# RWKV-6 attention and a squared-ReLU MLP in one kernel: source parity as row half of the score tiles, state in compact 64x64 tiles

## Chip, cores and metric

One core of one Trainium2 chip runs the whole kernel in one launch. The metric is the device time of an execution in microseconds (us), compared by medians of runs. Besides these times there is one profiled execution, from which the profile and the trace come.

## What is computed

For each batch and head a recurrence with a decay per token and channel, then an MLP over all tokens:

```python
B, H, S, D = 4, 8, 768, 48          # r, k, v, w: (B, H, S, D); u: (H, D)
for t in range(S):
    cur = einsum('bhd,bhe->bhde', u * k_t, v_t)
    y_t = einsum('bhd,bhde->bhe', r_t, state + cur)
    state = w_t[..., None] * state + einsum('bhd,bhe->bhde', k_t, v_t)
x = y.transpose(0, 2, 1, 3).reshape(3072, 384)
out = relu(x @ w_in) ** 2 @ w_out   # w_in: 384 x 2048, w_out: 2048 x 384, float32 in and out
```

## The kernel before

**Tiling.** Work goes in 12 steps `s` of 256 tokens: four batches of three steps each, so steps 0, 3, 6 and 9 begin with an empty state. A partition holds a pair of neighbouring tokens, with parity `j`, so a step is 128 pairs; they make two chunks `c` of 64 pairs (`Q`). Heads go in four pairs `p` of two heads `e`, each padded from 48 to 64 channels, so that a head pair fills 128 rows. A step's parts are loaded by `ld.s.x` (x is w, r, k or v, 384 KB each, four buffers for each part); `ld.g.i` and `ld.g.o` load the blocks of the two MLP weights, which `cast` turns to bf16.

**The operations of a step**, by their names in the program:
- `ww_`, `lw_`, `cum_`, `exp_`, `ac_`: the pair's decay, its logarithm (ScalarE), sums along the chunk by triangular matmuls on TensorE, exponentials, and each chunk's total decay. `rw_`, `kw_` multiply r and k by one token's decay; `rd_` multiplies r (i = 0) and k (i = 1) by the decays.
- `tr_` with `rkt_` (steps 0 to 3) or `dtr_` (steps 4 to 11) transpose them: by TensorE and a copy, or by a transposing DMA of SBUF. `rkT` holds both.
- `p_`: the scores, pairs of k against pairs of r, in 64x64 tiles of the array; `pm_` masks them on VectorE. Rows of a score tile are the 64 source pairs of chunk 0 and below them of chunk 1; the source parity `js` is a place in the free dimension.
- `su_` (k times v), `ts_` (adds the old state), `sn_` (multiplies by the decay): the state after each chunk. It is kept for a head pair as 128 rows by 96 columns, of which only the two diagonal blocks are wanted: zeros in `ac_buf` clear the others.
- `y_` (scores times v, in array tiles of 64 rows by 128 columns), `yc_` (r times the state, 128 by 64): the output in PSUM.
- `ku_`, `qp_`, `q_`, `vq_`: the term with u, a number q per token and head that multiplies v. It enters y through `yq_` (a matmul with `spread`) or, in steps 4 and 7 to 11, through `dvq`: four DMAs bring it to the output's layout, and `ysb_` adds it.
- `ysb_`, then `yt_` with `xt_` or the transposing DMA `dyt_`: the MLP's input `xT`.
- `m1_` (first layer, six matmuls of 256 columns, two PSUM banks in turn), `rl_` (ReLU), `sq_` (square), `m2_` (second layer, four of 384 columns), `os_` and `store`.

**Order.** All of it is written out in one string, `ORDER`; each engine carries out its own operations in the order in which they stand there. A word names the operation, the step, the PSUM banks after a colon, and after `=` the engine (A ScalarE, V VectorE, G GpSimd), where there is a choice. SyncE's queue (SP) issues all DMAs, loads, shuffles, transposes and stores, in that order too; an issue whose buffer or data isn't ready holds up those behind it. `warm_` words are matmuls of zeros for the time in which TensorE has nothing to do.

Of the kernel before, what the change touches and what calls it, by code (L numbers as in the profile page):

```python
# [29 lines left out]
rl_.0.5=A cast.o.1=V m2_.0.1.0:0 sq_.0.1=A cast.o.2=G cum_.3:1 q_.2 ld.3.v m1_.1.3:1 sq_.0.2=A pm_.2.0  # L30
m2_.0.0.0:1 vq_.2 sq_.1.3=A m2_.0.1.1 rl_.1.3=V m2_.0.1.2 ld.4.w v_.2=A sq_.1.1=V m1_.1.1:1 cast.o.3=A
m2_.0.0.1 rl_.1.5=V ld.4.r rl_.1.1=V m2_.0.0.2 ac_.3 m2_.0.0.3 rw_.3=V exp_.3 ld.4.k su_.2:0 sq_.1.0=A
os_.0.0=V m2_.0.1.3 ts_.2.0=V kw_.3=G rd_.3.0 m1_.1.4:0 os_.0.1=A ld.4.v m2_.1.0.0:1 sn_.2.0 rd_.3.1
m2_.1.0.1 v_.3=A ku_.3 tr_.3.0:0 ld.5.r rl_.1.4=A yy_.2:01 rkt_.3.0=V sq_.1.2=A ww_.4=V qp_.3 ld.5.k
tr_.3.1:0 ts_.3.0=V ysb_.2=A m2_.1.0.2 rkt_.3.1=V lw_.4 ld.5.w m2_.1.0.3 sn_.3.0 yt_.2:0 os_.1.0=A cum_.4:1
xt_.2=V rw_.4=G m2_.1.1.0:1 ac_.4 q_.3 exp_.4 m1_.2.2:1 kw_.4=G m1_.2.0:0 rd_.4.0 rl_.2.2=A m2_.1.1.1 ku_.4
rl_.2.0=A rd_.4.1 m1_.2.1:1 ts_.3.1=V m1_.2.3:0 dtr_.4.1 rl_.2.1=A v_.4=V vq_.3 pp_.3:10 rl_.2.3=A m2_.1.1.2
sq_.2.0=A ld.6.k pm_.3.0 m1_.2.5:1 ld.5.v sn_.3.1 pm_.3.1 ld.6.w m1_.2.4:0 rl_.2.5=A dtr_.4.0 m2_.1.1.3
sq_.2.1=A ww_.5=G m1_.2.6:1 os_.1.1=V rl_.2.4=A qp_.4 kw_.5=V yy_.3:10 sq_.2.2=A ld.6.r lw_.5 m2_.2.1.0:0
ysb_.3=A store.0.1 ts_.4.0=V m1_.2.7:0 q_.4 sn_.4.0 cum_.5:0 rl_.2.7=A yt_.3:1 rw_.5=V ld.7.w rl_.2.6=A  # L40
vq_.4 m2_.2.1.1 ac_.5 xt_.3=V m2_.2.1.2 exp_.5 ts_.4.1=V m1_.3.5:0 sq_.2.3=A rd_.5.0 ww_.6=G m2_.2.0.0:1
dvq.4 rl_.3.5=A rd_.5.1 m1_.3.1:1 m1_.3.0:0 rl_.3.1=V rw_.6=G pp_.4:10 rl_.3.0=A m1_.3.3:1 v_.5=A pm_.4.1
dtr_.5.0 ku_.6 m2_.2.0.1 lw_.6 rl_.3.3=A pm_.4.0 m2_.2.1.3 dtr_.5.1 m1_.3.7:0 ku_.5 m1_.3.4:1 ld.7.k
rl_.3.7=A yy_.4:01 store.0.0 rl_.3.4=A sn_.4.1 sq_.3.0=A ld.7.r m1_.3.6:0 ld.8.w qp_.5 ysb_.4=V os_.2.1=A
m1_.3.2:1 rl_.3.6=A ts_.5.0=V m2_.2.0.2 sq_.3.3=A rl_.3.2=V ld.6.v ww_.7=G yt_.4:0 q_.5 ld.8.r m2_.2.0.3
xt_.4=A kw_.6=G pp_.5:10 sq_.3.2=A m1_.4.1:0 pm_.5.1 qp_.6 store.1.0 m1_.4.3:1 rl_.4.1=A pm_.5.0 m2_.3.0.0:0
sq_.3.1=A ld.7.v cum_.6:0 kw_.7=G lw_.7 os_.2.0=V m1_.4.2:0 rl_.4.3=A rw_.7=V m2_.3.0.1 sn_.5.0 exp_.6
store.1.1 cum_.7:1 ac_.6 m2_.3.0.2 rd_.6.0 rl_.4.2=A vq_.5 m1_.4.0:1 exp_.7 rd_.6.1 m2_.3.0.3 ac_.7 v_.6=A
rd_.7.0 ku_.7 m1_.4.5:0 dtr_.6.1 rl_.4.0=A m2_.3.1.0:1 rd_.7.1 sq_.4.1=A m1_.4.4:1 dtr_.6.0 ww_.8=V qp_.7
os_.3.0=A yy_.5:01 q_.6 rl_.4.4=A ld.8.k sq_.4.0=A ld.9.w m1_.4.6:1 store.2.1 ysb_.5=V ts_.6.0=A m2_.3.1.1  # L50
sn_.6.0 ld.9.v rl_.4.5=V m2_.3.1.2 sq_.4.2=A ts_.6.1=V yt_.5:0 m1_.4.7:0 xt_.5=V sn_.6.1 lw_.8 m2_.3.1.3
rl_.4.7=V rl_.4.6=A kw_.8=G pp_.6:10 m1_.5.6:1 pm_.6.1 vq_.6 m2_.4.1.0:0 rl_.5.6=A pm_.6.0 m1_.5.4:0
os_.3.1=A ku_.8 v_.7=A store.3.1 m1_.5.0:1 rl_.5.4=V ld.8.v m2_.4.1.1 dtr_.7.0 yy_.6:01 qp_.8 ld.10.w
m1_.5.1:0 ts_.7.0=V ysb_.6=A dtr_.7.1 rw_.8=G m2_.4.0.0:1 sq_.4.3=A rl_.5.1=V m2_.4.0.1 sn_.7.0 q_.7 dyt_.6
rl_.5.0=A cum_.8:1 q_.8 m1_.5.3:0 vq_.7 exp_.8 ld.9.k m1_.5.7:1 ts_.7.1=V rl_.5.3=A ld.9.r rd_.8.0 m2_.4.0.2
ac_.8 v_.8=A m1_.5.2:0 rd_.8.1 dvq.7 rl_.5.7=A m2_.4.1.2 rl_.5.2=A m1_.5.5:1 sq_.5.1=V m2_.4.0.3 ww_.9=V
pp_.7:01 dtr_.8.0 rl_.5.5=V m1_.6.6:0 pm_.7.0 m1_.6.3:1 ku_.9 rl_.6.6=A ld.11.w m2_.4.1.3 pm_.7.1 store.3.0
rl_.6.3=A m1_.6.0:0 sq_.5.2=A dtr_.8.1 os_.4.1=V sn_.7.1 m1_.6.1:1 rl_.6.0=V sq_.5.0=A yy_.7:01 kw_.9=G
rl_.6.1=A lw_.9 rw_.9=G m1_.6.4:0 ts_.8.0=V ysb_.7=V m1_.6.5:1 qp_.9 rl_.6.4=A cum_.9:0 sq_.5.3=A rl_.6.5=V
dyt_.7 m2_.5.0.0:0 exp_.9 m1_.6.2:0 vq_.8 store.2.0 ac_.9 m2_.5.0.1 rd_.9.0 rl_.6.2=A ld.11.k m2_.5.0.2  # L60
ww_.10=G rd_.9.1 ld.10.r m2_.5.0.3 dvq.8 ww_.11=V m1_.6.7:1 os_.5.0=A sq_.6.2=V sq_.6.0=A pp_.8:10 rl_.6.7=V
m1_.7.1:0 os_.4.0=A m2_.5.1.0:0 lw_.10 rl_.7.1=V dtr_.9.0 m2_.5.1.1 q_.9 kw_.11=G m1_.7.7:1 dtr_.9.1 pm_.8.1
m1_.7.6:0 v_.9=G rl_.7.7=A m2_.6.0.0:1 lw_.11 sn_.8.0 pm_.8.0 ld.10.k rl_.7.6=A m1_.7.0:1 ld.11.r sq_.6.1=A
m1_.7.5:0 sq_.7.3=V sq_.6.3=A yy_.8:01 rl_.7.0=V rl_.7.5=V m2_.6.0.1 ysb_.8=V ts_.9.0=A m2_.5.1.2 sn_.9.0
# [26 lines left out]
def kernel(  # L91
# [13 lines left out]
    nc = tc.nc  # L105
# [475 lines left out]
```

## Time and profile before

| what | value |
|---|---|
| runs | 189.17, 192.50, 192.39 us; median 192.39 |
| profiled execution, first to last instruction (span) | 186.6 us; what lies around the span isn't in the profile: 5.8 us to the median |
| granted TensorE clock | 1.000 |
| busy: TensorE (PE), VectorE, ScalarE, GpSimd | 176.2, 133.7, 119.4, 103.7 us |
| DMA | 36.99 MB, mean 198 GB/s; 86.4% of 16 engines' span on SP's queue |
| first-layer matmuls (L478) | 576, 73.8 us busy |
| second-layer matmuls (L503) | 384, 72.1 us busy |
| score matmuls (L342) | 384 |
| output, carried and q*v matmuls (L395) | 384, 160 and 24 |
| state matmuls (L372) | 160 |
| DMA transposes `rkT<-rdec_buf` | 16, median 4.4 us from issue to landing |
| shuffles `vqs<-vq` | 24, median 3.6 us |

PE is TensorE's matmuls and PEld its weight loads, DVE is VectorE, ACT ScalarE, POOL GpSimd; L395 is line 395 of the kernel. Busy time is the union of the instructions' times; a matmul's duration has the passage through the array in it, so distances from start to start say more of what it costs. A line of the timeline or the chain merges neighbouring instructions of one kind.

### The profile page before, as it was taken

How to read it: one execution, taken by the hardware profiler on the slowest of the kernel's cores; microseconds unless marked ns; L12 is line 12 of the kernel's file. 1: busy time of each engine (PE TensorE's matmuls, PEld its weight loads, DVE VectorE, ACT ScalarE, POOL GpSimd, SP SyncE). 2: the span in 40 equal slices, each digit the busy share in tenths (PEclk: the TensorE clock that was granted, in tenths of full speed). 3: DMA queues.
4: the chain of work that ended last, by engine and by line, in shares of the span. 5: the costliest groups of instructions: out<-in, count | busy, mean ns of one | idle time of the engine just before them, and what ended most of it. 6: DMA issues, size and time to landing. Idle time of an engine off the chain costs nothing.

```text
span 186.6 us, 5415 instructions
## 1 busy us (share of the span) xinstructions
PE 176.2 (94%) x2284; PEld 125.4 (67%) x2284; DVE 133.7 (72%) x180; ACT 119.4 (64%) x193; POOL 103.7 (56%) x100
## 2 busy tenths in 40 slices
PE   7679979998999999999997999999999999999992
PEld 2245558865777778767766786777767877776661
DVE  4499927998589784889856958958996966705430
ACT  5447978988778877996747486738733073372431
POOL 7089944763999569995694595383673310000000
PEclk9999999999999999999999999999999999999999
DMA  6999999999998999999899999899497442403022
GB/s 151 269 282 354 317 213 345 364 313 259 243 239 192 167 284 174 280 286 172 236 208 184 236 216 255 142 191 254 144 130 169 100 109 63 87 0 126 0 88 85
DMA packets 80873, 36.99 MB, mean 198 GB/s; under 512 B 72529, under 2 KB 79313, under 8 KB 80849
## 3 DMA queue, kind: packets, MB, share of 16 engines
q1 hardware_dynamic: 80848, 36.64, 86.4%
q8 instruction: 18, 0.29, 0.7%
q14 instruction: 7, 0.05, 0.1%
HBM read 25.36 MB, written 4.72 MB: 161 GB/s over the span
## 4 chain that ended last, share of the span: by engine, by line
PE 68%; SPq 12%; DMA 8%; ACT 5%; DVE 2%; issue 1%; POOL 1%
PE bk L503 29%; PE m L478 27%; SPq L162 9%; PE att L395 5%; DMA w_st<-in_moe_w_out_dram 5%; DMA w_st<-in_moe_w_in_dram 4%; SPq L172 3%; PE att L342 3%; PE att L372 2%; ACT gt L487 2%; DVE q L274 1%; ACT v_bf L253 1%; ACT wo_sb L185 1%; POOL wi_sb L185 1%; SPq L190 1%
## 5 line engine op out<-in xcount | busy, mean ns | idle before, releaser
L478 PE MATMUL m<-xT,wi_sb 128*128 128x256 bf16 x576 | 73.8, 273 | 1.1 <-ACT gt L487 0.9
L503 PE MATMUL bk<-wo_sb,gt 128*128 128x384 bf16 x384 | 72.1, 326 | 0.6 <-ACT wo_sb L185 0.6
L478 PEld LDWEIGHTS <-wi_sb 128*128 128x128 bf16 x576 | 55.0, 98 | 14.0 <-issue 1.9
L487 ACT ACTIVATE gt<-m 128x512 f16<-128x512 f32 x57 | 33.5, 595 | 28.3 <-PE m L478 27.5
L503 PEld LDWEIGHTS <-gt 128*128 128x128 bf16 x384 | 36.9, 98 | 20.1 <-issue 0.8
L495 ACT ACTIVATE gt<-gt 128x1024 bf16<-128x1024 f16 x37 | 38.5, 1053 | 7.1 <-DVE gt L489 6.8
L489 DVE TENSOR_SCALAR gt<-m 128x512 f16<-128x512 f32 x39 | 26.2, 685 | 8.4 <-PE m L478 8.0
L355 DVE TENSOR_TENSOR pmT<-att,mask 128x1024 bf16<-128x1024 f32 x23 | 27.4, 1214 | 3.4 <-PE att L342 3.4
L265 POOL TENSOR_TENSOR ku<-k_raw,u_bc 128x768 f32<-128x768 f32 x12 | 22.1, 1848 | 9.7 <-DMA u_bc<-in_u_dram 5.0
L387 POOL TENSOR_TENSOR S<-t_state,ac_buf 128x384 bf16<-128x384 f32 x20 | 17.7, 886 | 9.9 <-ACT t_state L380 4.5
L270 POOL TENSOR_TENSOR ku<-ku,r_raw 128x768 f32<-128x768 f32 x12 | 22.3, 1864 | 0.5
L278 POOL TENSOR_TENSOR vq<-v_raw,q 128x768 bf16<-128x768 f32 x12 | 18.0, 1499 | 4.8 <-DVE q L274 4.8
L510 ACT ACTIVATE o_sb<-bk 128x384 f32<-128x384 f32 x15 | 7.3, 487 | 11.9 <-PE bk L503 11.9
L306 DVE TENSOR_TENSOR rdec_buf<-r_raw,att 128x768 bf16<-128x768 f32 x12 | 11.4, 949 | 3.0 <-ACT ac_buf L299 2.3
L520 PE MATMUL bk<-warm 128*128 128x512 bf16 x40 | 11.6, 424 | 1.2 <-DVE half_ones L213 1.2
L497 DVE TENSOR_TENSOR gt<-gt 128x1024 bf16<-128x1024 f16 x11 | 8.5, 773 | 5.0 <-ACT gt L487 5.0
L512 DVE TENSOR_SCALAR o_sb<-bk 128x384 f32<-128x384 f32 x9 | 5.0, 553 | 9.9 <-PE bk L503 9.9
L306 DVE TENSOR_TENSOR rdec_buf<-k_raw,att 128x768 bf16<-128x768 f32 x12 | 11.4, 947 | 0.5 <-ACT ac_buf L299 0.4
L274 DVE TENSOR_REDUCE q<-ku 128x16 f32<-128x768 f32 x12 | 11.1, 942 | 0.1
L261 POOL TENSOR_TENSOR k_raw<-k_raw,w_raw 128x384 f32<-128x384 f32 x7 | 7.2, 1022 | 6.9 <-DMA k_raw<-in_k_dram 5.9
L292 ACT ACTIVATE att<-att 128x768 f32<-128x768 f32 x12 | 9.6, 799 | 1.7 <-PE att L288 1.6
L342 PEld LDWEIGHTS <-rkT 64*64 64x64 bf16 x384 | 6.0, 106 | 5.2 <-issue 3.3
(75 smaller groups left out, 177.4 us busy)
## 6 DMA issues: line engine op xcount, KB each, us to landing
w_raw<-in_w_dram SPq DMA_DIRECT2D x12, 384.0 KB, 5.8
k_raw<-in_k_dram SPq DMA_DIRECT2D x12, 384.0 KB, 5.3
r_raw<-in_r_dram SPq DMA_DIRECT2D x12, 384.0 KB, 5.8
v_raw<-in_v_dram SPq DMA_DIRECT2D x12, 384.0 KB, 6.5
out_dram<-o_sb SPq DMA_DIRECT2D x24, 192.0 KB, 2.6
w_st<-in_moe_w_in_dram SPq DMA_DIRECT2D x4, 768.0 KB, 7.1
w_st<-in_moe_w_out_dram SPq DMA_DIRECT2D x4, 768.0 KB, 8.7
vqs<-vq SPq DMA_DIRECT2D x24, 48.0 KB, 3.6
```

The lines of the kernel that those rows point to most:

```text
L162: nc.sync.dma_start(out=t[:, :, at:at + 2, :].rearrange("p h j d -> p h (j d)"), in_=src[b, :, i * T:(i + 1) * T, :].rearrange("h (p j) d ...
L265: nc.gpsimd.tensor_mul(ku[:], raw["k", s][:, :, 1:3, :], u_bc[:, :, None, :].to_broadcast([C, H, 2, D]))
L270: nc.gpsimd.tensor_mul(ku[:], ku[:], raw["r", s][:, :, 0:2, :])
L278: nc.gpsimd.tensor_mul(vq[:].rearrange("p j h d -> p h j d"), raw["v", s][:], tiles.pop(("q", s))[:, :, :, None].to_broadcast([C, H, 2, D]))
L306: nc.vector.tensor_mul(rdec[:, i, :, :, 0:D], x.rearrange("p h j d -> p j h d"), cs[:, i, 0:DM].rearrange("p (h d) -> p h d", h=H)[:, None ...
L355: nc.vector.tensor_mul(pmT, ps_p[:].rearrange("p e (a x) -> p (e a) x", a=2), mk.to_broadcast([C, 4, 2 * C]))
L387: nc.gpsimd.tensor_mul(t[:], tiles.pop(("ts", s, c))[:].rearrange("p (a e d) -> p a e d", a=HP, e=2), tiles["a_c", s][:, :, c, :, None].to ...
L478: nc.tensor.matmul(ps1[:, j, :], wi_sb[:, n // 4, kk, n % 4 * 128:(n % 4 + 1) * 128], tiles["xT", s][:, :, kk, :], start=(kk == 0), stop=( ...
L487: nc.scalar.activation(rl, m1, AF.Relu, scale=RS)
L489: nc.vector.tensor_scalar(out=rl, in0=m1, scalar1=RS, scalar2=0.0, op0=ALU.mult, op1=ALU.max)
L495: nc.scalar.activation(gt, rl, AF.Square)
L503: nc.tensor.matmul(m2, gt[:, n, c * C:(c + 1) * C], wo_sb[:, n, :], start=(n == 0), stop=(n == NT - 1))
```

## The change

In steps 4 to 11 (`SHUFFLED`) the source parity becomes the row half of the score tiles: row half `js`, and chunk `c` in the free dimension. The output product then contracts over 128 rows (both parities) in full array tiles, with v in the same layout: v (bf16) and q stand in one tile of 800 bytes a row, which `dv_` brings by four DMAs to rows of (parity, pair); `vq_` multiplies them there, into float32. So r's transpose is laid out by chunk (`rT`), with r's DMA transpose split into two of 64 rows. In all steps the state is computed in 64x64 tiles for each head alone (192 columns a row instead of 384), and `sb_` copies it into a tile with zeros off the diagonal (`sb_bufs`), from which the carried product runs in full tiles for both output parities together. `ac_` becomes one instruction, `rd_` for r two, `exp_` can be halved, and `ku_`, `qp_`, `vq_` can run on either engine. All orders, engines and banks in `ORDER` are new. Two stretches of it, before and after, then the code:

```diff
-ld.0.w warm_.15.0 ld.1.w ld.0.k ld.0.r ld.0.u ld.1.r ww_.1=V ww_.0=V ld.1.k lw_.0 lw_.1 kw_.0=V cum_.0:0
...
+ld.0.w ww_.0=V lw_.0 warm_.18.0 cum_.0:0 exp_.0.1 ld.0.k kw_.0=G ld.0.r ld.0.u ld.1.w rd_.0.1 exp_.0.0
...
+warm_.2.2 y_.0:0 yq_.0 yc_.0 ysb_.0=A rd_.1.1 warm_.1.1 tr_.1.0:0 rkt_.1.0=V warm_.1.2 tr_.1.1:1 cast.i.3=A
+qp_.1=G rkt_.1.1=V sn_.0.1 ld.0.i v_.1=G yt_.0:0 cast.i.0=G ld.1.i xt_.0=A ld.2.w warm_.2.2 p_.1.0:0 p_.1.1:1
...
-vq_.4 m2_.2.1.1 ac_.5 xt_.3=V m2_.2.1.2 exp_.5 ts_.4.1=V m1_.3.5:0 sq_.2.3=A rd_.5.0 ww_.6=G m2_.2.0.0:1
-dvq.4 rl_.3.5=A rd_.5.1 m1_.3.1:1 m1_.3.0:0 rl_.3.1=V rw_.6=G pp_.4:10 rl_.3.0=A m1_.3.3:1 v_.5=A pm_.4.1
...
+ld.6.w ww_.6=V store.0.1 dtr_.4.0 m1_.3.4:0 dtr_.4.1 dv_.4 m1_.3.2:1 m2_.2.0.3 exp_.5 ld.6.r store.1.1 qp_.5=G
+rd_.5.0 v_.5=G rd_.5.1 ku_.6=G vq_.4=G rl_.3.4=A ac_.5 ts_.4.1=V rl_.3.2=A m1_.3.7:0 p_.4.1:0 p_.4.0:1 pm_.4.1
+pm_.4.0 rl_.3.7=A m1_.3.0:1 m2_.2.1.0:0 m1_.3.1:0 rl_.3.0=A sb_.4.0=A q_.5 m1_.3.5:1 os_.2.0=V y_.4:0 yc_.4
+ysb_.4=V rl_.3.1=A rl_.3.5=A dtr_.5.1 m1_.3.6:0 m2_.2.1.1 rl_.3.6=A dtr_.5.0 p_.5.0:1 sn_.4.1 sb_.4.1=V lw_.6
+su_.5:m p_.5.1:0 yt_.4:1 qp_.6=G xt_.4=A ld.8.w sq_.3.0=A ts_.5.0=V m1_.3.3:0 m2_.2.1.2 m2_.2.1.3 os_.2.1=A
+rw_.6=G m1_.4.3:1 sn_.5.0 pm_.5.1 pm_.5.0 ld.7.w ld.7.r rl_.4.3=V dv_.5 ld.6.v sb_.5.0=A kw_.6=G cum_.6:0
...
+SHUFFLED = range(4, 12)
...
+    sb_bufs = [consts.tile([C, HP, 2, D], BF16, name=f"sb_buf{i}") for i in range(NSB)]
...
+    def dv_(s):
+        v = tiles["v32", s]
+        vs = tiles["vs32", s] = a_mid.tile([C, 2, (DM + QT) // 2], FP32, name="v_sh")
+        tiles["vs", s] = vs[:].bitcast(BF16)
+        for j in range(2):
+            for c in range(2):
+                nc.sync.dma_start(out=vs[j * Q:(j + 1) * Q, c, :], in_=v[c * Q:(c + 1) * Q, j, :])
...
     def vq_(s):
+        if s in SHUFFLED:
+            vs = tiles["vs", s]
+            vq = tiles["vqs", s] = a_mid.tile([C, 2, H, D], FP32, name="ku", bufs=3)
+            q = tiles["vs32", s][:, :, DM // 2:]
+            nc.gpsimd.tensor_mul(vq[:], vs[:, :, 0:DM].rearrange("p c (h d) -> p c h d", h=H),
+                                 q[:, :, :, None].to_broadcast([C, 2, H, D]))
+            return
...
     def dtr_(s, i):
-        nc.sync.dma_start_transpose(
-            out=new_rkt(s, i)[:, i].rearrange("p j a t -> p (j a) t"),
-            in_=tiles["rdec", s][:, i].rearrange("t j h d -> t (j h d)"))
+        t = new_rkt(s, i)
+        if i == 0:
+            rdec = tiles["rdec", s][0][:].rearrange("t a j e d -> t (a j e d)")
+            for c in range(2):
+                nc.sync.dma_start_transpose(out=t[:, c], in_=rdec[c * Q:(c + 1) * Q])
+        else:
+            nc.sync.dma_start_transpose(out=t[:].rearrange("p j a t -> p (j a) t"),
+                                        in_=tiles["rdec", s][1][:].rearrange("t j h d -> t (j h d)"))
...
     def p_(s, f):
...
                     for c in range(2):
-                        rows, part = slice(e * DP, (e + 1) * DP), slice(c * Q, (c + 1) * Q)
-                        at = a * 256 + js * 128
-                        nc.tensor.matmul(half[part, at:at + C], rkT[rows, 1, js, 2 * f + a, part],
-                                         rkT[rows, 0, :, 2 * f + a, part], start=True, stop=True)
+                        rows, pair = slice(e * DP, (e + 1) * DP), 2 * f + a
+                        if s in SHUFFLED:
+                            part, at = slice(js * Q, (js + 1) * Q), a * 256 + c * 128
+                        else:
+                            part, at = slice(c * Q, (c + 1) * Q), a * 256 + js * 128
+                        nc.tensor.matmul(half[part, at:at + C], kT[rows, js, pair, c * Q:(c + 1) * Q],
+                                         rT[rows, c, 2 * pair:2 * pair + 2, :], start=True, stop=True)
...
     def su_(s):
...
-                for c in range(n_c):
-                    part = slice(c * Q, (c + 1) * Q)
-                    nc.tensor.matmul(ps_su[c][:, p * 2 * D:(p + 1) * 2 * D],
-                                     rdec[part, 1, j, 2 * p:2 * p + 2, :], v_bf[part, 2 * p:2 * p + 2, j, :],
-                                     start=(j == 0 and p == 0), stop=(j == 1), skip_group_check=True)
+                for e in range(2):
+                    for c in range(n_c):
+                        part, h = slice(c * Q, (c + 1) * Q), 2 * p + e
+                        nc.tensor.matmul(ps_su[c][e * DP:(e + 1) * DP, p * D:(p + 1) * D],
+                                         kdec[part, j, h, :], v_bf[part, j, h * D:(h + 1) * D],
+                                         start=(j == 0 and p == 0), stop=(j == 1), skip_group_check=True)
...
+    def sb_(s, c):
+        t = tiles["S", s + c, 1 - c]
+        b = tiles["sb", s + c, 1 - c] = sb_bufs[(2 * s + c - s // NB) % NSB]
+        copy = dict(A=nc.scalar.copy, V=nc.vector.tensor_copy, G=nc.gpsimd.tensor_copy)[where["sb_", s, c]]
+        for e in range(2):
+            rows = slice(e * DP, (e + 1) * DP)
+            copy(b[rows, :, e, :], t[rows])
...
     def y_(s):
...
+                if s in SHUFFLED:
+                    for c in range(2):
+                        y_mm(s, c, cols, pmT[:, p // 2, 2 * e + p % 2, c, :], tiles["vs", s][:, c, cols])
+                    continue
...
     def yc_(s):
         for c in range(0 if s % NB else 1, 2):
             for p in range(HP):
-                for j in range(2):
-                    y_mm(s, c, slice(2 * p * D, (2 * p + 2) * D),
-                         tiles["rkT", s][:, 0, j, p, c * Q:(c + 1) * Q],
-                         tiles["S", s, c][:, p].rearrange("p e d -> p (e d)"), j)
+                y_mm(s, c, slice(2 * p * D, (2 * p + 2) * D),
+                     tiles["rT", s][:, c, 2 * p:2 * p + 2, :].rearrange("p j t -> p (j t)"),
+                     tiles["sb", s, c][:, p].rearrange("p e d -> p (e d)"))
```

More of the change, by code (lines that the diff above doesn't have):

```diff
@@ L43 @@
[L43 to L52, printed above, removed]
@@ L87 @@
+os_.11.0=A store.11.0
 """
+SHUFFLED = range(4, 12)
 @with_exitstack
@@ L239, with sh_ @@
     tiles = {}
+    def sh_():
+        for js in range(2):
+            rows = slice(js * Q, (js + 1) * Q)
+            nc.scalar.copy(mask_sh[rows, 0, :], tri_strict[rows, rows])
+            if js == 0:
+                nc.scalar.mul(mask_sh[rows, 1, :], tri_incl_neg[rows, rows], -1.0)
+            else:
+                nc.scalar.copy(mask_sh[rows, 1, :], tri_strict[rows, rows])
     def ww_(s):
@@ L408, in y_ @@
                         part = slice(c * Q, (c + 1) * Q)
-                        y_mm(s, c, slice(h * D, (h + 1) * D),
-                             pmT[part, p // 2, 2 * e + p % 2, js, :], v_bf[part, h, js, :])
-    def dvq(s):
-        vq = tiles.pop(("vq", s))
-        vqs = tiles["vqs", s] = a_mid.tile([C, 2, DM], BF16, name="vqs")
-        for j in range(2):
-            for c in range(2):
-                nc.sync.dma_start(out=vqs[j * Q:(j + 1) * Q, c, :],
-                                  in_=vq[c * Q:(c + 1) * Q, j].rearrange("p h d -> p (h d)"))
+                        y_mm(s, c, cols, pmT[part, p // 2, 2 * e + p % 2, js, :], v_bf[part, js, cols])
     def yq_(s):
@@ L519, in warm_ @@
         for _ in range(n):
-            nc.tensor.matmul(bk[i][:], warm[:, 0:C], warm[:], start=True, stop=True)
+            nc.tensor.matmul((bk + m1_bank)[i][:], warm[:, 0:C], warm[:], start=True, stop=True)
     def ld(n, x):
```

254 lines of the change are left out of this document (148 added, 106 removed).

## The prediction

> **What bounds the kernel now.** I read the busy times and slices of the page first, then the windows, the chain, PE's timeline and SP's timeline.
>
> ```profile
> PE 176.2 (94%) x2284; PEld 125.4 (67%) x2284; DVE 133.7 (72%) x180; ACT 119.4 (64%) x193; POOL 103.7 (56%) x100
> ...
> PE   7679979998999999999997999999999999999992
> ...
> PEclk9999999999999999999999999999999999999999
> DMA  6999999999998999999899999899497442403022
> ```
>
> PE is busy in nearly every slice at full clock, and the DMA engines are full until slice 30 (about 140 us). The windows (PE, PEld, DVE, ACT and POOL busy in 10 us; clock; DMA share; GB/s) show that no other engine is:
>
> ```profile
> 60.00:70.00 10.00, 10.00 (x156) 7.31 (x151) 8.24 (x11) 7.99 (x14) 6.27 (x6) 1.00 1.23 230
> 70.00:80.00 10.00, 10.00 (x163) 7.80 (x162) 7.04 (x9) 8.86 (x13) 10.00 (x9) 1.00 1.24 231
> 90.00:100.00 10.00, 9.99 (x157) 7.48 (x158) 7.18 (x10) 5.75 (x10) 9.02 (x7) 1.00 1.06 206
> ```
>
> A piece of the chain (start, length, what) gives PE's prices:
>
> ```profile
> 119.20 1.31 PE m L478 x12
> 120.51 0.45 PE att L372 x16
> 120.96 0.86 PE att L395 x48
> 121.81 1.41 PE bk L503 x8
> 123.22 1.31 PE m L478 x12
> 124.53 0.57 PE att L342 x32
> 125.10 0.76 PE bk L503 x4
> 125.86 0.66 PE m L478 x6
> ```
>
> Twelve first-layer matmuls take 1.31 us (109 ns each), four second-layer ones 0.65 (162 ns). But the four after the scores take 0.76: 0.11 us goes with the change of array tile (64x64 to 128x128). Start by start in PE's timeline a change of tile shape costs 90 to 97 ns either way; I use 95. Leaving these and the warm-up out, I count 162.7 us of needed PE work: 62.8 first layer, 62.4 second, 5.1 cumulative sums, 5.5 transposes, 5.28 scores, 4.37 state updates, 4.95 output products, 3.49 carried products, 1.98 for q*v, and 72 changes of shape, 6.84. The other 23.9 us of the span: 8.6 of warm-up matmuls, 1.2 before the first matmul, about 8.1 of gaps until 43.3 us, 1.4 of gaps later, 3.6 after the last matmul starts, the rest rounding. After 43.3 us PE hardly waits, so PE's work from there on is time.
>
> **PE's terms.** From the starts in its timeline:
> - Scores. Now four 64x64 tiles run together: four matmuls start within 10 ns, the next four 56 ns later, 32 in 0.44 us. From step 4 the inner loop (chunk c) stays on one tile and only e and the parity change it. Two in a row on one tile must follow each other (the eight L372 matmuls of steps with one chunk, all on one tile, take 43 ns each; those on two tiles 23). Whether the pair holds up the other row half is seen here (start, length, what):
>
> ```profile
> 71.23 0.42 PE L372 MATMUL att<-v_bf,rdec_buf 64*128 64x96 bf16 x6
> 71.46 0.19 PE L395 MATMUL att<-v_bf,pmT 64*128 64x48 bf16 x1
> 71.50 0.20 PE L372 MATMUL att<-v_bf,rdec_buf 64*128 64x96 bf16 x1
> ```
>
>  The output matmul on rows 64 to 127 starts at 71.46, before the last two state matmuls on rows 0 to 63 that stand ahead of it in the program. Row halves thus have queues of their own, and each half keeps its two column tiles fed, with one extra 55 ns per call: 0.55 a step instead of 0.44, over eight steps +0.9 us. If instead nothing is lost: 0; if order is strict, 16 follow-ups of 56 to 58 ns, 0.91 a step: +3.8.
> - State updates: twice as many (320), on four 64x64 tiles. No row has 48 columns there. A weight load of 64 columns shows as 26 ns at the start of the carried products and the scores, so a round of four is 27 ns, eight rounds 0.22 us a step: 2.64 for 4.37, -1.7. Worst: 13.7 ns each as scores have, no gain; best 25 ns a round, -2.0.
> - Output: 32 half-row matmuls (pairs each 25 ns, 0.41 us) become 16 full ones. Nearest row: the four 128x128 matmuls with 2 columns (L285) start 25 ns apart, and 48 columns stream in about 20: 0.40 us, -0.1 in all. Worst is the transpose's 55.5 ns: +3.8.
> - Carried products: 16 at 22 ns become 8 at 42 (as L372 on one tile): -0.1. q*v matmuls leave steps 5 and 6: -0.7.
> - Changes of shape: now five a step (two round the scores, three round update, output and carry). Afterwards output and carry are 128x128 like the MLP, only scores and updates leave it, some side by side. Counting through both orders: 72 becomes 43: -2.8.
>
> Sum: -4.5 us; with all ends, from -5.7 to +4.0.
>
> **The start.** All orders are new. Step 0 goes ahead of step 1, and the first-layer weights move up: the last of the four is the 14th load instead of the 17th. With before's landing intervals (1.5 us a step load, 2.05 a weight block; first landing 4.4) it lands at 25.5 instead of 31.2. I added up step 0 op by op: decay 4.4 to 5.0, log, sums after the warm-up at 6.5, exponentials, products and transposes, scores at 12.1 and 13.1, masks until 15.2, output, xT at 20.1, first m1 at 20.9 (now 24.7). DVE sets it for step 1, xT at 28.0. By 28.1 PE then has done 12.7 us of needed work; now 28.1 less 8.6 of warm-up, 1.2 and 6.9 of gaps, so 11.4. That is 1.3, and a 0.7 us wait for the last second-layer weights at 43.3 shrinks (they move up too; cover: 13 us of first-layer work): **-1.5**. Bounds: -3 if the later gaps close as well, +1 if DVE, with 13.2 us of work set in PE's second ten (8.8 now), is late.
>
> **Other engines.** By rows, with sizes halved where tiles are: sn_ on POOL 0.89 to about 0.45 (20), ts_ on DVE 0.55 to about 0.34; new: sb_, two copies each, 0.6 on ACT (11) or 0.4 on DVE (9), estimates between the 64x64 copy (0.24) and 128x384 (0.5); v_ goes to POOL (0.82, 9 times); ten more squares on DVE. Totals: DVE +2, ACT -9, POOL +3. I cost them at nothing: ACT sat 27.5 us waiting for first-layer results, POOL has 44% free. DVE's cover is thin: 92 to 95 us of work set before PE's hundredth microsecond, of some 102 available.
>
> **SP and DMA.** Here the change adds work and waits:
>
> ```profile
> 59.40 2.75 SPq L327 DMA_TRANSPOSE rkT<-rdec_buf  x1
> ...
> 65.31 2.80 SPq L418 DMA_DIRECT2D vqs<-vq  x4
> 68.22 2.63 SPq L327 DMA_TRANSPOSE rkT<-rdec_buf  x2
> ```
>
> Each step from 4 on issues three transposes instead of two (r's as two of 64 rows) and four shuffles of v with q, in all eight steps instead of six. A transpose holds SP 1.25 us at best, the four shuffles 2.4. And y now waits for v's shuffle (first issue to last landing was 4.5 to 6.1 us for vqs); behind y on PE stands the MLP, and behind that wait vq on POOL and ysb on DVE. SP's issues from step 4's first transpose to step 8's shuffle come to 42.7 us at their shortest, with 53 us from PE's places. First miss: step 5's transposes follow products ready at about 57.1 of PE's work; SP ends their issue at 60.9, the last lands 3.1 us (shortest) after its issue starts at 59.7: 62.8, and scores stand at 61.2: 1.6 late (2.9 with the median 4.4). Later steps are about even.
> The flow itself: back to back, landings are 1.45 us apart for a step load, about 1.1 for a transpose and for four shuffles, 0.5 a store. Up to step 8's shuffle that makes 101.3 us now, landed at 119.1: 0.87 of the time from 3 us on; up to 57.2 us it was 0.93. Afterwards it is 102.6 if a half transpose takes half (0.55), 108.1 if a full 1.1, and PE wants it at 112.8. At 0.93 and the half price it is there at 113; at 0.87 and the full price at 127.3, 14.5 late. No row has a half transpose; I take the half, as bytes go, and the 1.6 us of step 5, which covers the flow's 0.2. Bounds: 0 to 14.5.
>
> **Sum.** 186.6 - 4.5 - 1.5 + 1.6 = 182.2 us of span. The median of the runs shown is 192.4, 5.8 over the profiled span (fastest 189.2, 2.6 over); I keep 5.8: **188.0**, 2.3% under.
>
> **Rivals.**
> - *No new wait*: SP runs ahead far enough, since 26 instead of 23 step loads stand before its first transpose. 186.6 - 6.0 + 5.8 = 186.4.
> - *DMA flow late, not fatal*: half price at 0.87, 121 instead of 112.8, 8 late: 194.4. For it: SP spent 55 us on 54 issues between 55 and 117 us, three fifths over their shortest times. Against: part of that is slack that PE never missed.
> - *DMA flow becomes the bound, slower*: half transposes cost as many packets as whole ones and so the full 1.1 us, at 0.87: 14.5 late, 186.6 - 6.0 + 14.5 + 5.8 = 200.9. It turns slower than before by over 2% once y's input is 9.9 us late. For it: DMA share over 1 already, in the windows. Against: 0.93 was reached.
> - *DVE the bound* from 10 to 100 us: some 3 us more waiting, 191.0.
> - *Scores in strict order*: +3.8 instead of +0.9, 190.9. The Trainium skill (TensorE: Matmul & The Clock Gate, Part 3, "The mechanism") states that matmuls start and end strictly in program order, which would give this; the trace disagrees at 71.46 us, so little chance.
>
> **Chances.** Forecast 0.33 (its own range 185.5 to 190.5; 0.26 faster, 0.07 within), no new wait 0.21 (faster), late flow 0.11 (within), flow the bound 0.29 (slower), DVE 0.03 and strict order 0.03 (within). Together 0.47 faster by over 2%, 0.24 within, 0.29 slower; 2% is about what a measurement of this kernel can tell from no change. The range goes from 184.5 (the start's better end) to 198.5, half into the slower rival.
>
> **What would show it.** Right: scores of steps 4 to 11 near 0.55 us, updates near 0.22, outputs 25 ns apart, about 156 to 159 us of needed PE work, first m1 near 21 us, PE waiting a microsecond or two between 60 and 75 us for rT, kT or v_sh. Wrong: long PE waits for these from 60 to 115 us, half transposes landing as far apart as whole ones, pairs of scores 56 ns apart, outputs above 30 ns, or first m1 later than 24 us.

## The result, and the profile after

The changed kernel takes **202.03 us** (median of four runs, 201.07 to 202.56) against 191.25 (189.17 to 192.50) of the kernel before on the same chip: ratio 1.0629, 95% interval 1.0562 to 1.0696. It is slower by 6%; 188.0 had been predicted, with 198.5 as the upper end. The profiled execution took 201.57 us, its span 199.8 (before 186.6). Ratios leave disturbed runs out, so they can differ a little from the quotient of two medians.

The page, in the lines that were shown of before:

```profile
PE 177.2 (89%) x2229; PEld 125.0 (63%) x2229; DVE 154.8 (77%) x215; ACT 111.9 (56%) x200; POOL 112.2 (56%) x107
...
PE   7997986699999687979797979979999989999993
...
PEclk9998799999999999999999999999999999999999
DMA  6999999998999139999999989798756470132022
```

PE's row now has sixes and sevens from 30 to 40 us and on and off from 65 to 135, where it had nines. DVE is busy for 21 us more than before, not the 2 of the prediction; some 18 of them lie in instructions that took longer than the fastest of their kind (added up further below). The DMA row has a hole: its fourteenth digit (65 to 70 us) is a 1. The DMA engines have no more work: 81.2% of 199.8 us on SP's queue is 162 us, before 86.4% of 186.6 us, 161. The windows that were shown of before:

```profile
60.00:70.00 10.00, 8.29 (x183) 5.46 (x182) 9.63 (x14) 6.88 (x12) 7.34 (x7) 1.00 0.86 109
70.00:80.00 10.00, 8.34 (x111) 6.54 (x111) 9.11 (x13) 5.25 (x11) 9.77 (x8) 1.00 0.78 136
90.00:100.00 10.00, 8.54 (x128) 6.39 (x127) 7.39 (x12) 5.67 (x9) 7.06 (x6) 1.00 1.32 217
```

PE (the first of the five) falls from 10.0 to 8.3, DVE (the third) rises to 9.6. From 10 to 100 us DVE is busy for 80.6 us (before 73.6), PE for 77.1 (before 86.7). The chain in the worst stretch (start, length, what):

```profile
64.97 1.04 DVE gt L580
66.00 0.93 DVE sb_buf L481
66.94 0.35 DVE sb_buf L481
67.29 1.44 issue
68.73 0.95 DVE v_bf L311
69.68 0.26 DVE t_state L466
69.94 0.48 DVE xT L546
70.42 0.04 issue
70.46 1.47 PE m L561 x12
71.93 0.65 PE bk L586 x4
72.58 0.65 PE m L561 x6
73.24 0.58 PE att L418 x32
```

PE waits 2.3 us, until 70.46, for xT, which DVE copies last. Ahead of it stand the two copies of `sb_`. In VectorE's and GpSimd's timelines they look like this:

```profile
65.93 2.79 DVE L481 COPY sb_buf<-S 64x192 bf16<-64x192 bf16 x2
68.73 0.95 DVE L311 TENSOR_REDUCE v_bf<-ku 128x16 f32<-128x768 f32 x1
```

```profile
65.41 1.46 POOL L285 TENSOR_TENSOR r_raw<-r_raw,w_raw 128x384 f32<-128x384 f32 x1
66.83 1.82 POOL L296 TENSOR_TENSOR ku<-k_raw,u_bc 128x768 f32<-128x768 f32 x1
```

A copy of 64x192 takes 0.19 to 0.21 us when GpSimd rests. Here the first ends with `r_raw` (66.9) and the second with `ku` (68.7). And behind q (`v_bf L311`) waits SP, in whose timeline nothing is issued from 64.1 to 69.8 us; that is the hole in the DMA row:

```profile
60.15 2.62 SPq L399 DMA_TRANSPOSE rT<-rdec_buf  x2
62.87 1.26 SPq L401 DMA_TRANSPOSE kT<-kdec_buf  x1
69.75 2.45 SPq L320 DMA_DIRECT2D v_sh<-v_bf  x4
```

The work on PE came out as reckoned. In steps 4 to 11, where nothing interrupts them, the 32 scores of a step start within 0.44 us (0.43 before); in the chain, with a change of tile shape in it, such a piece has 0.58 to 0.65. The state updates

```profile
60.48 0.37 PE att L456 x32
...
109.58 0.26 PE att L456 x32
...
134.24 0.40 PE att L486 x16
```

0.26 to 0.37, sixteen outputs 0.40 (25 ns each). PE's needed work, added up from starts as in the prediction, is some 160 us (before 162.7); the gaps between its instructions rose from 9.5 to 26.3 us.

### The profile page after: what moved, and what is told of

The parts are those of the page before. It is cut to its first block, busy times and chain, and to the rows that moved or that the text cites. A ratio compares the mean times of both kernels' runs of the same rounds, so it can differ in the third digit from the quotient of the medians.

```text
span 199.8 us, 5395 instructions
## 1 busy us (share of the span) xinstructions
PE 177.2 (89%) x2229; PEld 125.0 (63%) x2229; DVE 154.8 (77%) x215; ACT 111.9 (56%) x200; POOL 112.2 (56%) x107
## 2 busy tenths in 40 slices
DMA packets 81767, 37.43 MB, mean 187 GB/s; under 512 B 72912, under 2 KB 80208, under 8 KB 81744
## 3 DMA queue, kind: packets, MB, share of 16 engines
q1 hardware_dynamic: 81744, 37.10, 81.2%
## 4 chain that ended last, share of the span: by engine, by line
PE 48%; DVE 22%; DMA 14%; issue 6%; SPq 4%; ACT 2%; POOL 2%; DVEq 0%; POOLq 0%
PE m L561 18%; PE bk L586 18%; DMA xT<-y_sb 5%; DMA v_sh<-v_bf 4%; PE bk L603 4%; DVE gt L580 3%; DMA rT<-rdec_buf 3%; DVE sb_buf L481 3%; SPq L320 3%; DVE r_raw L285 2%; DVE rdec_buf L362 2%; PE att L486 2%; DVE kdec_buf L365 2%; PE att L418 2%; DVE gt L572 2%
## 5 line engine op out<-in xcount | busy, mean ns | idle before, releaser
L578 ACT ACTIVATE gt<-gt 128x1024 bf16<-128x1024 f16 x27 | 28.1, 1051 | 2.8 <-DVE gt L572 2.7
L471 POOL TENSOR_TENSOR S<-t_state,ac_buf 128x192 bf16<-128x192 f32 x20 | 11.0, 552 | 29.3 <-DVE t_state L466 21.8
L580 DVE TENSOR_TENSOR gt<-gt 128x1024 bf16<-128x1024 f16 x21 | 22.9, 1097 | 3.5 <-ACT gt L570 3.2
L426 DVE TENSOR_TENSOR pmT<-att,mask_sh 128x1024 bf16<-128x1024 f32 x16 | 19.0, 1218 | 2.4 <-PE att L418 2.3
L327 POOL TENSOR_TENSOR ku<-v_sh 128x768 f32<-128x768 bf16 x8 | 11.8, 1479 | 8.1 <-DMA v_sh<-v_bf 8.1
L365 DVE TENSOR_TENSOR kdec_buf<-k_raw,att 128x768 bf16<-128x768 f32 x12 | 11.3, 946 | 3.1 <-ACT att L347 3.0
L347 ACT ACTIVATE att<-att 128x768 f32<-128x768 f32 (+1 forms) x14 | 9.9, 709 | 5.2 <-PE att L342 4.1
L481 DVE COPY sb_buf<-S 64x192 bf16<-64x192 bf16 x18 | 12.3, 686 | 0.1
L362 DVE TENSOR_TENSOR rdec_buf<-r_raw,att 128x384 bf16<-128x384 f32 x24 | 12.1, 543 | 0.0
L265 POOL TENSOR_TENSOR ww<-w_raw 128x384 f32<-128x384 f32 x8 | 9.2, 1148 | 4.5 <-DMA w_raw<-in_w_dram 4.5
```

Of the source, the lines that this page charges most:

```text
L426: nc.vector.tensor_mul(tiles["pmT", s][:, f].rearrange("p a c t -> p (a c) t"), ps_p[:].rearrange("p e (x t) -> p (e x) t", x=4), mask_sh[ ...
L481: copy(b[rows, :, e, :], t[rows])
L578: nc.scalar.activation(gt, rl, AF.Square)
L580: nc.vector.tensor_mul(gt, rl, rl)
```

## The experiments

Two suspects came out of this: **A**, VectorE, through its waits for GpSimd, and **B**, SP and the DMA engines, with the shuffles and the half transposes; **C** holds that the way through a step is just longer. (D and L, later, split B: SP's queue of issues, or the shuffle's place.) Each ratio is against the kernel before on the same chip; the kernel after has 1.0629.

**1. `sb_` on ScalarE** (e1).

```diff
-sb_.1.0=V sb_.1.1=V sb_.2.0=V sb_.3.1=V sb_.4.1=V sb_.7.0=V sb_.7.1=V sb_.9.0=V sb_.10.1=V
+sb_.1.0=A ...
```

> The changed kernel with the nine sb_ copies that stand on VectorE moved to ScalarE, in place. Theory A (VectorE is the bound from 10 to 75 us, because copies and products that read and write SBUF alone wait there until GpSimd's running instruction ends): VectorE loses all 12.3 us of sb_, 8.9 of it waiting, and some of GpSimd's 10 us of stretching goes too; the chain had 6.2 us of sb_; 195 to 198 us instead of 202. Theory B (the DMA flow and SP's queue, with more transposes and shuffles, are the bound): the queues are as they were, 200.5 to 203 us. Theory C (the longer path of each step, sb_ and the shuffle in it, whatever the engine): a copy on ScalarE is 0.35 us, so 201 to 203 us.

195.79 us (195.05 to 196.44), ratio 1.0209 [1.0129, 1.0288]: as A expected. Nine pairs of small copies are worth 6.2 us. PE's gaps fell to some 22 us.

**2. The squares as well** (e3): the 15 `sq_` of steps 0 to 8 that VectorE had also go to ScalarE.

> As the kernel with sb_ on ScalarE, and also the 15 squares of steps 0 to 8 that stand on VectorE moved to ScalarE (1.05 us each there). Theory A: VectorE loses 15 squares with 8.7 us of waiting in them, ScalarE has 40 us of waiting for the first layer to fill; 188 to 193 us, so about as before. Theory B: 200.5 to 203 us. Theory C: 201 to 204 us, since a square on ScalarE is 0.37 us longer than a free one on VectorE.

204.77 us (201.47 to 206.59), ratio 1.0558 [1.0417, 1.0698]: A missed. VectorE fell to 125.8 us busy, and added up over its groups its instructions took only 6.3 us more than the fastest of their kind (23.5 in the kernel after), yet by the two ratios some 7 us were lost against e1. The list of waits shows one that had been small in e1 (0.5 and 0.2 us):

```profile
PEld L586 <- ACT gt L578: 6.5, 6, 2.6
PE bk L586 <- ACT gt L578: 4.3, 4, 2.4
```

(engine and line, whom it waited for: us in all, times, the longest.) The second layer now waits for squares that stand in ScalarE's queue, 2.6 us at once. A less loaded VectorE is worth nothing if what it was relieved of stands at the wrong place of another engine's order.

**3. No shuffles** (e5): `vs = tiles["vs32", s] = v` instead of the four `dma_start` of `dv_`.

> The changed kernel without the 32 DMAs of dv_: y_ and vq_ read v and q from the tile that dv_ would have shuffled, so the rows of v are in the wrong order in steps 4 to 11. Theory B: 19 us of SP's issues and 1.6 MB of DMA are gone, the waits of PE for v_sh too (3.3 us at 87, 102 and 120 us) and with the flow ahead those for rT: 192 to 196 us. Theory A: VectorE is as full as before until 75 us; only PE's waits for v_sh and SP's wait of 5.6 us for step 4's q go: 198 to 201 us. Theory C: the path is shorter by some 5 us a step: 193 to 198 us.

197.75 us (196.31 to 198.57), ratio 1.0304 [1.0213, 1.0395]. That is above B's range, just below A's and inside C's: the shuffles matter, but are not the whole.

**4. A strided source for `sb_`** (e7).

```diff
-t = tiles["S", s + c, 1 - c] = a_mid.tile([C, HP, D], BF16, name="S", bufs=4)
+t = tiles["S", s + c, 1 - c] = a_mid.tile([C, HP, D, 2], BF16, name="S", bufs=4)[:, :, :, 0]
```

> The changed kernel with the state tile S written to every second bf16 element (twice as wide in SBUF), so that sb_ on VectorE, still there with its nine pairs of copies, reads with a stride. Theory A: if a strided read keeps the copy from the mode that has to wait for GpSimd, the copies take 0.2 to 0.35 us instead of 0.69 on average, VectorE's busy time falls by 6 to 8 us, and the time to 196 to 199 us; if the copies still last up to 1.8 us, the stride does not matter and the time stays. Theory B and C: 200.5 to 203 us whatever the copies last.

201.69 us (200.56 to 204.19), ratio 1.0494 [1.0364, 1.0624]. The copies take 0.24 to 0.26 us alone and up to 1.88 with GpSimd at work: the stride doesn't free them.

**5. The disputed cost by itself** (x1, one execution): the copies and squares, first with GpSimd idle, then while it runs four multiplications.

> Computes nothing of the reference: six short series of one instruction, each first with GpSimd idle and then while GpSimd runs four multiplications of 128x768 float32 one behind the other. The series: the copy that sb_ makes (64x192 bfloat16, SBUF to SBUF) on VectorE; the same from a source of stride 2; the same from PSUM; the same copy on ScalarE; the square (128x1024); a float32 copy 128x384. Theory A (VectorE's instruction on SBUF waits until GpSimd's running one has ended, and then holds GpSimd back): copies 0.19 to 0.21 us alone, and with GpSimd the first of each pair waits for the rest of a multiplication, 0.7 to 1.7 us; squares 0.69 alone, 1.2 to 2.2 with GpSimd; copies from PSUM and on ScalarE the same in both. Rival (the two engines share the bandwidth of SBUF): everything that touches SBUF is longer by one ratio, at most 2, ScalarE's copies and VectorE's reads from PSUM too.

The timeline, the second of each pair with GpSimd at work:

```profile
4.51 3.73 DVE L56 COPY sb_buf<-S 64x192 bf16<-64x192 bf16 x16
...
8.81 10.22 DVE L56 COPY sb_buf<-S 64x192 bf16<-64x192 bf16 x16
...
9.41 7.43 POOL L51 TENSOR_TENSOR pool_out<-pool_a,pool_b 128x768 f32<-128x768 f32 x4
...
36.34 6.15 DVE L56 CAST sb_buf<-ps 64x192 bf16<-64x192 f32 x16
...
43.18 6.16 DVE L56 CAST sb_buf<-ps 64x192 bf16<-64x192 f32 x16
...
51.64 5.95 ACT L56 COPY sb_act<-S 64x192 bf16<-64x192 bf16 x16
...
57.72 5.95 ACT L56 COPY sb_act<-S 64x192 bf16<-64x192 bf16 x16
...
65.70 4.32 DVE L63 TENSOR_TENSOR gt<-rl 128x1024 bf16<-128x1024 f16 x6
...
70.46 10.38 DVE L63 TENSOR_TENSOR gt<-rl 128x1024 bf16<-128x1024 f16 x6
```

Sixteen copies go from 3.73 to 10.22 us: during the four multiplications just four get through, 1.77 to 1.85 us each, one per multiplication. From PSUM nothing changes (6.15, 6.16), nor on ScalarE (5.95). Strided copies (4.53 to 10.94), float32 copies (3.15 to 9.08) and squares (4.32 to 10.38) wait as well. GpSimd's multiplications kept their time beside the bfloat16 copies and grew, all four together, to 8.41 us beside the squares. So it is a wait for the running instruction, not shared bandwidth.

**6. Both remedies** (e8): e1 and no shuffles.

> The kernel after with sb_ on ScalarE and without dv_'s 32 transfers (steps 4 to 11 multiply v in the wrong row order). If the two are separate losses (VectorE held by GpSimd, and the way of v_sh through SP and the DMA engines), their gains add: 202.0 - 6.2 - 4.3 = 191.5, 190 to 193, the time of before. If both lie on one chain and the second only takes up what the first had freed, 194 to 196, what sb_ on ScalarE alone gave.

190.29 us, ratio 0.9986 [0.9910, 1.0062]: the losses add, and without them the kernel stands where it was before.

**7. v on ScalarE too** (e9): e1, and `v_.1` to `v_.9` from G to A.

> sb_ on ScalarE, and the nine v_ of GpSimd (0.77 us each, 6.9 us) on ScalarE too. With sb_ on ScalarE the chain runs through GpSimd without a break from 40.7 to 75.2 us (ku, r_raw, v_bf, k_raw), and it is GpSimd that holds VectorE. Theory A with GpSimd as the next bound: 192 to 194, and VectorE's excess over its own fastest falls below the 15.0 us of sb_ on ScalarE alone. Rival (ScalarE's in-order queue: what is put in front of relu and exp delays them, as with the squares): 196 to 199.

200.33 us (198.22 to 204.40), ratio 1.0454 [1.0258, 1.0651]: the way the rival said, with a median above its range. ScalarE's `v_bf` now waits 12.7 us for v's loads (3.8 in e1), and relu and exponentials queue behind it.

**8. The copies in the kernel before** (b1): nine times two copies to a spare tile ahead of `yc_`.

> The kernel before, with what sb_ puts on VectorE in the kernel after added to it: nine times two copies of 64x192 bfloat16 from S to a spare buffer that nothing reads, placed ahead of the carried products of the same step. Theory A: 3.6 us of VectorE work that with the waits for GpSimd takes about 12 us (1.4 a pair), in a kernel whose VectorE has 92 to 95 us of work before TensorE's hundredth: 194 to 198. Rival C (the loss lies in the longer path per step, not on the engine): nothing reads these copies, so no path is longer, and the time stays at 190.5 to 193.

192.48 us (191.39 to 194.99), ratio 1.0136 [0.9911, 1.0360]. The medians are level, as C had it, but the interval takes in A's lower end: inconclusive. The copies did wait, with 0.659 us each on average. That they cost so little here may be because before has 16.5 us of VectorE idle between 10 and 100 us to take them, and after only 9.4; no run tests that.

**9. Stores issued by ScalarE** (e11): e1, with `nc.scalar.dma_start` in the 17 stores behind ScalarE's `os_`.

> sb_ on ScalarE, and the 17 stores whose o_sb ScalarE writes are issued by ScalarE, right behind that instruction, instead of by SP (0.43 to 0.6 us each, 7 to 10 us of SP). Theory D (SP's queue, 9.4 to 9.7 us of every 10 taken from 10 to 110 us, is what the transposes and v_sh wait in): 192 to 194. Theory L (the shuffle costs by its place: the products wait for the 4 us from its issue to its last landing, wherever SP stands): 195 to 197, as with sb_ on ScalarE alone (195.8). Above 197: ScalarE's own queue pays for the issues.

194.92 us (193.72 to 197.86), ratio 1.0145 [1.0059, 1.0231]: between the ranges of D and L, and not told apart from e1. SP's issues added up to 142 us instead of 146, but SP, with its waits, still had 9.0 to 9.6 of every 10 us taken from 50 to 110.

**10. Whole transposes of r** (e13): e1, with one transposing transfer instead of two.

> sb_ on ScalarE, and rT of steps 4 to 11 by one transposing transfer of 128 rows instead of two of 64 (the blocks of r lie in the wrong places, so its scores are those of other rows; sizes and waits are the same). It takes 8 x 1.25 = 10 us off SP and puts the last landing some 0.5 us closer to the first. Theory D: 192 to 194. Theory L: 194.5 to 196, for the halves are at most 0.5 us apart. My prediction had put this part at 1.6 us: 194.2.

191.86 us (189.85 to 193.96), ratio 1.0005 [0.9946, 1.0064]. D, and more than it promised: 3.9 us. The bytes moved are the same (37.43 MB); the DMA engines were busy for 158.5 us instead of 162.4.

**11. All three** (e12): e1, no shuffles, whole transposes.

> sb_ on ScalarE, no dv_ (v in the wrong row order in steps 4 to 11), and the whole transpose of r (blocks in the wrong places): what is left of the change is the work on TensorE, full tiles and compact state. If the three are the whole of what the prediction had not seen, its own sum is left: 188.0 less the 1.6 it gave for the transposes, 186 to 188. If the transposes cost nothing beside the other two, 190.3 as without them; a remainder above that would be a further cause (the start, where the first product of the network came at 23.0 instead of 20.9).

190.61 us, ratio 0.9958 [0.9912, 1.0003], no better than without the shuffles alone (190.29, 0.9986). The shuffles (5.5 us after e1 by the medians, 4.3 by the ratios) and the halves (3.9) thus do not add: I read them as two ways of relieving one thing, and either relief is nearly enough.

**12. SP's queue in the kernel before** (b2): 32 transfers of 32 bytes.

```diff
+        if i == 0:
+            for _ in range(4):
+                nc.sync.dma_start(out=extra_out.pop()[0:1], in_=extra_in[0:1])
```

> The kernel before with 32 transfers of 32 bytes each from SBUF to SBUF, four behind each transpose of r in steps 4 to 11; nothing reads them. They take SP's queue some 0.57 us each, 18 us in all, as much as the kernel after adds there (154.6 us against 136.4), and almost none of the DMA engines' time. Theory D: SP has 86 of the 110 us from 50 to 160 taken, so 18 us more fill it: 195 to 200. Theory L: 191 to 193, for nothing that is waited for comes more than a transfer's issue later.

204.00 us (202.13 to 205.82), ratio 1.0606 [1.0504, 1.0709]: D, and past its end. One kilobyte of transfers that nothing reads costs as much as the whole change. In the timeline of its SP, its DMA row, and its waits:

```profile
61.90 2.62 SPq L330 DMA_TRANSPOSE rkT<-rdec_buf  x1
64.56 3.56 SPq L335 DMA_DIRECT2D extra<-extra_in  x4
...
72.98 2.10 SPq L330 DMA_TRANSPOSE rkT<-rdec_buf  x1
75.13 2.75 SPq L335 DMA_DIRECT2D extra<-extra_in  x4
```

```profile
DMA  6999999999939494994998929739755363131122
```

```profile
PEld L348 <- DMA rkT<-rdec_buf: 8.7, 4, 3.3
PE att L348 <- DMA rkT<-rdec_buf: 7.5, 4, 2.9
```

An issue of 32 bytes holds SP 0.65 us in the median, one of a 50 KB shuffle (kernel after) 0.59. SP's issues add up to 154 us (before 133, after 148; the 136 and 155 of the expectation have SP's waits for semaphores in them), the DMA engines run dry (the fours and twos in the row), and the scores wait for transposes, which in the kernel before they never did.

**13. Same load, other link** (e14): ScalarE makes `sb_`, and VectorE repeats the nine in place to a spare tile.

> The nine sb_ that the kernel after has on VectorE are made by ScalarE, and VectorE makes the same copies, in the same places of its order, into a spare buffer that nothing reads. VectorE thus has the whole load of the kernel after, its waits for GpSimd too; only the link from the state to the carried products is ScalarE's. If VectorE's time (and what stands behind the copies in its order: q, and with it SP's issue of v_sh) is the loss: 200 to 203. If the link itself is the loss: 195 to 197, as with sb_ on ScalarE alone (195.8). The same copies in the kernel before cost nothing that could be measured, which speaks for the second; SP's wait of 5.6 us for q behind two copies at 66 us speaks for the first.

**14. The same places without the wait** (e16): `nc.vector.reduce_sum(sb_spare[rows, e], t[rows], axis=AX.X)` instead of the spare copy.

> As the run before it with the copies into a spare buffer (202.1), but each of the 18 spare copies on VectorE is a sum over the last axis of the same 64x192 values. In the kernel after VectorE's sums (q, 0.940 to 0.955 us) are never longer while GpSimd runs, so these should take some 0.25 us each whatever GpSimd does, where the copies had 0.2 alone and up to 1.8 with it. The places in VectorE's order and the work are the same or a little more; only the waiting for GpSimd is gone. If that waiting is what makes sb_ on VectorE dear: 195 to 197.5, as with sb_ on ScalarE alone. If it is VectorE's order (a copy in place waits for GpSimd to have made the state, and all behind it with it): 200 to 203.

e14: 202.11 us (200.87 to 203.14), ratio 1.0678 [1.0597, 1.0760]. e16: 196.60 (195.84 to 197.35), ratio 1.0301 [1.0187, 1.0415]. The two groups (busy us, mean ns of one, idle time before them):

```profile
L485 DVE COPY sb_spare<-S 64x192 bf16<-64x192 bf16 x18 | 14.0, 776 | 0.1
```

```profile
L485 DVE TENSOR_REDUCE sb_spare<-S 64x4 f32<-64x192 bf16 x18 | 6.2, 342 | 0.1
```

So the 6 us do not lie in a longer link to the carried products (C): copies that nobody reads bring the loss back whole. Nor do they lie in the places in the order or in the work: the sums are longer than an undisturbed copy (0.34 against 0.2 us), stand in the same places, don't wait for GpSimd (0.33 to 0.35 us each), and most of the loss is gone. It is the waiting.

**15. SP's relief elsewhere** (e15): e11, with the loads of w and v from step 4 on issued by ScalarE. **16.** The same in the kernel before (b3).

> sb_ on ScalarE; the 17 stores behind ScalarE's own o_sb and the 16 loads of w and v from step 4 on issued by ScalarE instead of SP. A store took ScalarE 0.34 to 0.38 us; 33 issues make 12 us of ScalarE, and take 17 to 29 us off SP. Theory D (SP's queue is what transposes and v_sh wait in): 190 to 193, about as without the second half transposes or without the shuffles. Rival (ScalarE's queue pays, or the loads crowd the DMA engines earlier): 195 to 198.

> The kernel before with the same relief of SP: stores behind ScalarE's o_sb, and the loads of w and v from step 4 on, issued by ScalarE. If SP's queue already sets time in the kernel before (32 tiny transfers on it cost 12.4 us), 187 to 190; if the queue has just room enough there, 190.5 to 193, for TensorE's gaps lie before 50 us, where these issues do not stand.

e15: 206.64 us (204.56 to 207.54), ratio 1.0891 [1.0779, 1.1003], D missed. The waits say why:

```profile
POOL ww L265 <- DMA w_raw<-in_w_dram: 15.0, 3, 8.6
```

(GpSimd waits for the loads of w.) In the kernel after this was 4.5 us in all. SP runs ahead of the other engines and so issues loads early; ScalarE reaches the same word of the order later, the load lands 8.6 us late, and ScalarE's logarithm waits for it with relu behind. b3: 191.24, ratio 1.0094 [1.0051, 1.0137]: no gain either. Moving the issue also moves its time, so this run doesn't measure SP's room.

## Why the prediction was wrong, by its steps

**PE's terms: nearly right.** From start to start, scores took 0.45 us a step (0.55 said, 0.44 before), updates 0.26 (0.22), outputs 25 ns, needed work 160 us (158.2). Row halves did not hold each other up at all, so the extra 0.9 us for the scores did not come. Some 3 of the 4.5 us came; that they are what brings the kernel without the three losses level with before is likely, but no run shows it.

**The other engines: here it failed.** "I cost them at nothing", with DVE +2. It was +21. `sb_` on DVE was put at 0.4 us a pair and took 1.37 (12.3 us in nine pairs); a square had 0.77 in the kernel before and 1.10 after. The groups after, and the squares before (busy us, mean ns of one, idle time before them):

```profile
L481 DVE COPY sb_buf<-S 64x192 bf16<-64x192 bf16 x18 | 12.3, 686 | 0.1
L580 DVE TENSOR_TENSOR gt<-gt 128x1024 bf16<-128x1024 f16 x21 | 22.9, 1097 | 3.5 <-ACT gt L570 3.2
L497 DVE TENSOR_TENSOR gt<-gt 128x1024 bf16<-128x1024 f16 x11 | 8.5, 773 | 5.0 <-ACT gt L487 5.0
```

Added up over the groups, what DVE's instructions took above the fastest of their kind was 5.3 us before and 23.5 after. The rival in which DVE is the bound from 10 to 100 us named the place, but with 3 us and a chance of 0.03; e1 gives 6.2, e14 against e1 6.3 and against e16 5.5. The sentence "DVE's cover is thin" was right and led to no price. The row that should have given it was in the trace of before: squares of 0.68 us when GpSimd rested and 1.30 when it ran. The Trainium skill (SBUF — State Buffer, "SBUF: two separate sides") states that VectorE, with two SBUF inputs or in a two-port mode, and GpSimd lock a shared pair of ports for a whole instruction, and the other one waits. Run x1 agrees: one copy of 1.77 to 1.85 us for each multiplication of 1.80. In e16 the sums, which have one input, did not wait.

**SP and DMA: the sign was right, the thing and the size were not.** The term was 1.6 us, on SP's shortest issues (42.7 us of 53), and the large rival (200.9) was a flow of packets that is full. The flow was not full: the DMA engines had 162 us of work against 161, they ran dry, and the halves of the one transpose of r with both landings in the trace landed 0.5 us apart (107.36, 107.86), so the half price held there. Yet PE, for which the list of waits of before has none for a DMA, now waits for shuffles and transposes (us in all, times, the longest):

```profile
PE att L486 <- DMA v_sh<-v_bf: 2.8, 2, 1.5
PE att L418 <- DMA rT<-rdec_buf: 2.7, 3, 1.3
PEld L418 <- DMA kT<-kdec_buf: 2.0, 3, 1.0
```

What was nearly full was SP's queue: with its waits it was taken for 8.4 to 9.7 of every 10 us from 10 to 110 (before 6.7 to 9.7). The share alone is no sign of loss, for in e13 it is 9.1 to 9.7; and 5.6 us of one stretch, 60 to 70 us, are the wait for q. The shuffles, or else the half transposes, cost 4 to 5.5 us, and b2 shows that issues alone can cost as much, though in the kernel before. In the kernel after no run relieves the queue and leaves the transfers as they are with a gain (e11 and e15 had none), so that it is the issue and not the transfer that costs there is likely, not shown. I had read "three fifths over their shortest times" as slack; 32 issues more took all of it and 12 us. That the rival's 200.9 is close to the result is chance.

**The start: wrong.** First m1 came at 22.92, not 20.9. Part of that is this execution: with the same order up to there it came at 21.5 to 21.6 in e3, e5 and e14, where the granted clock was 1.00 from 10 to 30 us (here 0.94, then 0.89). The clock is not all of it either, for e8 had 1.00 and 23.1. Until 43 us PE's gaps are 11.4 us (before 8.1). The two largest, 1.25 at 31.45 and 2.21 at 36.48, wait for DVE (a weight cast, `kdec`); with `sb_` on ScalarE the second shrinks to 0.33. So in this execution about 3 us of loss instead of 1.5 of gain, part of it the same cause.

**The sum.** 186.4 (the forecast without its transposes) + 5.2 (SP: e1 less e12) + 6.2 (`sb_`) = 197.8. The last 4.2 us to 202.0 are by construction the distance of e12 from 186.4, not a cause that was found; e12's larger PE gaps lie at the start and, about a microsecond each, where the second layer waits for squares. How much of that is squares waiting for GpSimd stays open: taking them off VectorE (e3) brought another loss. No version tried beats the kernel before.

## What to carry to other kernels

Price a copy or a product on VectorE that works from SBUF to SBUF by GpSimd's running instruction, not by its own length; put small copies on ScalarE, or read from PSUM, where GpSimd is busy much of the time (here 56% of the span) and VectorE is nearly full. In b1, where VectorE had more idle time, such copies waited too and cost nothing that could be measured. Treat the queue that issues DMAs as an engine with its own busy time: count issues, not bytes, at their usual length, and ask what a transfer that moves nothing would cost. Work that is moved to relieve an engine brings its wait into another engine's order; three of the five such moves here (squares, v, loads) lost more than they freed, one (stores) gave next to nothing, and only the small copies paid.

## What the runs showed of the hardware that I had not expected

VectorE's copy of 64x192 bfloat16 in SBUF takes 0.2 us alone and up to 1.85 while GpSimd multiplies, with a stride of 2 too, and float32 copies likewise; its sums over the last axis (0.34 us, and 0.94 for q) and its copies from PSUM (0.35 to 0.36 us in x1) did not stretch in any of these runs. A DMA issue of 32 bytes held SP 0.65 us in the median, a transposing one 1.26 of 64 rows (kernel after) and 1.28 of 128 (e13); a store issued by ScalarE held that engine 0.34 to 0.38 us.
